# Two filter blocks transposed by their load instead of on TensorE, and one norm taken from PSUM, in a convolution-plus-FFN kernel

## The chip, the core and the metric

The kernel runs on one core of a Trainium2 chip. The metric is the time of one execution in device microseconds. The engines are TensorE (PE; its weight loads are PEld), VectorE (DVE), ScalarE (ACT), GpSimd (POOL) and SyncE (SP). SP and POOL also issue DMAs: SP's go through a hardware queue, POOL's through a software queue.

## The reference, cut to what matters

Sequence length S = 2048, width D = 640, FFN width F = 1728, everything bf16 in memory.

```python
h  = x + conv(layernorm(x), k, v)          # x is A_q
h2 = h + ffn(layernorm(h))

def conv(q, k, v):
    k_shift = causal 4-tap filter of k along S, per channel (shift_k)
    kv = k_shift * v
    y  = causal convolution of kv with ssm_k, per channel (a length-2S FFT in the reference)
    return q * (y + kv * ssm_D)

def ffn(x):
    return (silu(x @ w_gate) * (x @ w_up)) @ w_down
```

`ssm_k` is stored as [640, 2048], channels first. Its transform needs it with the sequence on the partitions, so each of its four blocks of 512 positions is transposed somewhere.

## The kernel before, in words

The sequence is cut into four blocks of N = 512 rows. For each block i the kernel forms kv (`kv`), transforms it with cosine and sine tables on TensorE (`xfwd`, tiles `X`, and `FO` for the odd half), multiplies it in the frequency domain with the filter blocks' transforms `C` (`prod`, VectorE, sums in `Y`), transforms back (`inverse`), normalises, and runs the FFN (`ffn`; for blocks 0 and 3 the gate and up products are in `gates`).

The four filter blocks come first. `kload(m)` loads block m as `kc[m]`, channels on the partitions. `ktrans(m)` transposes it on TensorE: two tasks of ten 128 x 128 transposes with the identity (L570), each followed by one eviction of 1280 columns from PSUM into `KT[m]`. `kfwd(m)` transforms `KT[m]` (L612); its results, even half in `C` or `R` and odd half in `KO`, are combined by VectorE butterflies (L583).

`kv(i)` loads K transposed with a transposing DMA (`tload`, L516, tile `kT`), applies the four taps with matmuls whose weights are the diagonal tiles `dg` and `dl` (L714, L719), and evicts. For block 0 it transposes back on TensorE (L733) and VectorE multiplies straight from PSUM into `vt` (L738). For the other blocks five more transposing DMAs make `kvo` and VectorE multiplies from there (L750). `dg` and `dl` are made by VectorE (L552, L556) from the identity and from `wcol`, the taps, which ACT's queue loads.

The second layernorm stands in `inverse`. For blocks in `ST` (0 to 2) one fused VectorE operation reads the inverse transform from PSUM, adds a row statistic, multiplies with x and sums (L876); POOL scales the sum (L880) and ScalarE squares and sums (L882). For block 3 ScalarE evicts from PSUM (L886), VectorE multiplies (L889), and ScalarE sums (L900) and squares (L902). All then use POOL for the power (L913). The normalised tile is transposed into `hnT` by four DMAs (L516), which the FFN's matmuls need.

The order of the work is written out by a table of numbers: `ORDER` holds, for each engine and for SP's queue, the numbers of the tasks in the order in which they are issued. Every engine works strictly in that order, and a task waits on semaphores for the tasks it depends on. PSUM tiles come from four units in turn. `VECTOR` lists the evictions that VectorE does instead of ScalarE, and `FILL` puts filler matmuls ahead of a task.

Of the kernel before, what the change touches and what calls it, by code (L numbers as in the profile page):

```python
# [10 lines left out]
ALU = mybir.AluOpType  # L11
# [11 lines left out]

class _Task:
    __slots__ = ("eng", "fn", "cost", "lat", "deps", "after", "succ", "npred", "ready", "end", "start",
                 "opens", "tiles", "idx", "clock", "sem", "seq", "dma", "name", "gap", "lock", "fill", "late", "pause", "alt")


class _Tile:
# [29 lines left out]
class _Graph:  # L59
# [38 lines left out]
    def add(self, eng, name, fn, cost, r=(), w=(), pr=(), pw=(), skip=(), lat=None, dma=None, after=(), lock=None):  # L98
        t = _Task()
# [131 lines left out]
    def emit(self, block):  # L231
# [5 lines left out]
        for t in self.glob:  # L237
# [32 lines left out]
            if t.dma is not None:  # L270
                t.sem = es.enter_context(nc.semaphore("s_d%d" % nd))
                nd += 1
                t.clock[t.sem] = 16
                prog[t.eng].append(lambda e, t=t: t.fn(e).then_inc(t.sem, 16))
            else:
                t.clock[t.eng] = t.idx
                prog[t.eng].append(lambda e, t=t, h=sems[t.eng]: t.fn(e).then_inc(h, 1))
        for t in self.glob:
            if t.dma is not None and not t.succ:
                prog["sp"].append(lambda e, t=t: e.wait_ge(t.sem, 16))  # L280

        @block.gpsimd
        def _(g):
# [23 lines left out]

ORDER = {
    "pe": """
# [7 lines left out]
    """,  # L317
    "act": """
# [11 lines left out]
    """,  # L330
    "dve": """
# [10 lines left out]
    """,  # L342
    "pool": """
        8 10 5 9 6 11 7 151 209 212 195 198 216 202 219 205 134 135 339 417 401 420 393 409 404 396 412 528 621 605 597 613
        624 600 608 616 770 775 780 785 732 827 809 836 818
    """,
    "sp": """
# [3 lines left out]
    """,  # L351
}

FILL = "20:6 313:8"

VECTOR = """
    59 83
"""

def bass_sequential_preLN__ssm_conv_h3__swiglu_ffn__prompt_kernel(  # L360
# [38 lines left out]
    with ExitStack() as es:  # L399
# [17 lines left out]
        NU = 5  # L417
# [8 lines left out]
        IE = sb("IE", o + 10400, [2, 2, D])  # L426
        o += 15520
        T = sb("T", o, [NU, 2, D])
        o += NU * 2560 - 10240
        kvo = sb("kvo", o + 10240, [4, D])  # L430
        FO = sb("FO", o + 10240, [2, 2, D])
# [16 lines left out]
        GA = sb("GA", o, [NC5, FA * P])  # L448
        UA = sb("UA", o + 8960, [NC5, FA * P])
        o += 17920  # L450
        GB = sb("GB", o, [NC5, FBK * P])
        UB = sb("UB", o + 7680, [NC5, FBK * P])
        PK = sb("PK", o + 15360, [NC5, P])
# [14 lines left out]
        epc = sb("epc", o + 544, [4], f32)  # L468
        assert o + 576 <= SBB + 16481 - A0, o + 576

        BN, DIRECT, D8, PT, BN2, ST, R4, PAIR, WARM, ACC, EA, KD, RD, LA, RA, HALF = (0,), (), (), (0,), (), (0, 1, 2), ('xf2',), True, 24, ((1, 3), (2, 3)), True, (2, 3), (), (1, 2, 3), (0, 1, 2), (0, 3)
        g = _Graph(nc, es)

        def cpe(n, k):
# [5 lines left out]
        def cdve(n):  # L480
            return 69 + n / 1.92
# [28 lines left out]
        def load(name, dst, src, nbytes, eng="sp", late=0, **kw):  # L510
            return g.add(eng, name, lambda e: e.dma_start(dst, src), 450, w=[dst], dma=(nbytes / 345.0, 0), lat=1900 + late, **kw)
# [24 lines left out]
        if WARM:  # L536
# [4 lines left out]
            def spin(e, pt=pt):  # L541
# [14 lines left out]
        g.add("dve", "dl", lambda e: e.tensor_tensor(out=dl[:], in0=id128, in1=w128, op=ALU.mult), 650,  # L556
              r=[wcol[:], ident[:]], w=[dl[:]])
# [4 lines left out]
        def ktrans(m):  # L562
            for jj in range(2):
                pt = g.tile("kt")

# [197 lines left out]

        ring_t = list(range(NU))
        ZB = sb("ZB", S[7], [2, 2, 2, D])

        def pair(u, v):
            return bass.AP(T[:].tensor, T[:].offset + 2 * D * u, [list(T[:].ap[0]), [D, 2], [(v - u) * 2 * D, 2], [1, D]])

        def prod(j, i):  # L770
            cm, nm = C[i - j], "p%d%d" % (j, i)
            for f2 in range(2):
                y = Y[:, f2]
                s = slice(f2, f2 + 3, 2)
                x, k = XH[j][:, s], cm[:, s]
                ksw = bass.AP(k.tensor, k.offset + D, [list(k.ap[0]), [4 * D, 2], [-D, 2], [1, D]])
                u = [ring_t.pop(0) for _ in range(4)]
                t1, t2 = pair(u[0], u[1]), pair(u[2], u[3])
# [382 lines left out]
```

## Time and profile before

| | |
|---|---|
| three runs | 262.37, 265.21, 268.7 us; median 265.21 |
| the profiled execution | 261.53 us, its span 259.5 us |
| granted TensorE clock | 1.0 |
| busy share of the span | PE 97%, PEld 65%, DVE 77%, ACT 75%, POOL 14% |
| first FFN matmul of block 0 | 55.96 us after the span's start |
| last filter matmul | up to 53.9 us |
| first inverse matmul of block 3 | 195.42 us |
| first FFN matmul of block 3 | 212.22 us |

Times in the views are microseconds from the span's start. The span is what the engines' instructions cover; the time of the execution is 2.0 us longer. The profiled execution is one of its own, 3.7 us below the median of the three runs. A busy share is an average over stages with different limits, so the busy time is better read stage by stage.

### The profile page before, as it was taken

To read this page: it belongs to the slowest core of one execution; us is meant where nothing else is said; L and a number is where in the kernel's file an instruction comes from. 1 tells how busy PE (TensorE), PEld (TensorE's weight loads), DVE (VectorE), ACT (ScalarE), POOL (GpSimd) and SP (SyncE) were. 2 spreads that over 40 slices of the span, in tenths; PEclk is the share of its full clock that TensorE was granted. 3 is DMA by queue.
4 is the path that set the end of the run, shared out by engine and by line. 5 is a ranking of instruction groups with operands and counts; after the bars stand their busy time and mean duration, and the time that the engine had idled before them with its cause. 6 is when DMAs were issued, how large, how long until landed. Compare 5 with 4: busy or idle time off the path is not lost.

```text
span 259.5 us, 4704 instructions
## 1 busy us (share of the span) xinstructions
PE 252.9 (97%) x1900; PEld 168.4 (65%) x1900; DVE 201.0 (77%) x292; ACT 194.8 (75%) x372; POOL 37.3 (14%) x49
## 2 busy tenths in 40 slices
PE   8999979999999999999999999999999999999996
PEld 5657645567888756644445666444456678888764
DVE  0799999999999999999999999999997010231222
ACT  2889999995698989669867798658977987654220
POOL 0001000434012141000030170310140101000000
PEclk9999999999999999999999999999999999999999
DMA  6995997999999653430031314993500030300005
GB/s 174 336 339 138 315 254 94 378 172 220 248 139 189 115 143 73 106 126 4 1 81 20 104 47 79 202 226 54 105 0 0 3 76 0 54 1 3 0 3 177
DMA packets 44792, 31.13 MB, mean 120 GB/s; under 512 B 32353, under 2 KB 41442, under 8 KB 44770
## 3 DMA queue, kind: packets, MB, share of 16 engines
q1 hardware_dynamic: 41968, 25.58, 38.9%
q0 software_dynamic: 2144, 5.24, 11.3%
q8 instruction: 15, 0.25, 0.4%
q10 hardware_dynamic: 658, 0.01, 0.1%
q14 instruction: 7, 0.06, 0.1%
HBM read 15.69 MB, written 2.62 MB: 71 GB/s over the span
## 4 chain that ended last, share of the span: by engine, by line
PE 86%; DMA 7%; ACT 5%; DVE 1%; SPq 0%; issue 0%
PE ps L1048 21%; PE ps L943 19%; PE ps L985 11%; PE ps L986 11%; PE ps L612 9%; PE ps L862 6%; DMA PK<-in_B_w_up_dram 3%; DMA kc<-in_A_ssm_k_dram 2%; PE ps L719 2%; DMA vt<-in_A_v_dram 2%; PE ps L1030 1%; ACT KT L504 1%; PE ps L1060 1%; ACT FO L504 1%; ACT X L504 1%; PE ps L649 1%
## 5 line engine op out<-in xcount | busy, mean ns | idle before, releaser
L1048 PE MATMUL ps<-Wd,GU 128*128 128x384 bf16 (+1 forms) x390 | 55.8, 299 | 0.0
L1048 PEld LDWEIGHTS ps<-Wd,GU 128*128 128x128 bf16 x390 | 37.9, 98 | 15.6 <-issue 0.5
L943 PE MATMUL ps<-hnT,GA 128*128 128x256 bf16 x140 | 31.1, 272 | 0.0
L943 PE MATMUL ps<-hnT,UA 128*128 128x256 bf16 x140 | 31.1, 273 | 0.0
L965 DVE TENSOR_TENSOR GU<-GU,ub 128x512 bf16<-128x512 bf16 (+1 forms) x28 | 10.9, 402 | 25.6 <-ACT GU L961 16.9
L781 DVE TENSOR_TENSOR T<-X,C 128x2560 bf16<-128x2560 bf16 x20 | 29.7, 1486 | 0.1
L782 DVE TENSOR_TENSOR T<-X,C 128x2560 bf16<-128x2560 bf16 x20 | 29.7, 1486 | 0.1
L943 PE MATMUL ps<-hnT,GB 128*128 128x256 bf16 x120 | 26.9, 273 | 0.5 <-DMA PK<-in_B_w_up_dram 0.5
L943 PE MATMUL ps<-hnT,UB 128*128 128x256 bf16 x120 | 26.9, 273 | 0.0
L961 ACT ACTIVATE GU<-ps 128x512 bf16<-128x512 f32 (+1 forms) x28 | 15.5, 568 | 14.8 <-PE ps L943 13.0
L985 PE MATMUL ps<-hnT,GA 128*128 128x512 bf16 x70 | 26.5, 379 | 0.0
L986 PE MATMUL ps<-hnT,UA 128*128 128x512 bf16 x70 | 26.5, 379 | 0.0
L1010 ACT ACTIVATE ub<-ps 128x512 bf16<-128x512 f32 (+1 forms) x30 | 17.1, 569 | 11.7 <-PE ps L986 6.3
L985 PE MATMUL ps<-hnT,GB 128*128 128x512 bf16 x60 | 22.7, 379 | 0.0
L986 PE MATMUL ps<-hnT,UB 128*128 128x512 bf16 x60 | 22.7, 379 | 0.0
L612 PE MATMUL ps<-KT,ftab 128*128 128x320 bf16 x128 | 19.5, 300 | 1.5 <-ACT KT L504 1.4
L963 ACT ACTIVATE ub<-ps 128x512 bf16<-128x512 f32 (+2 forms) x32 | 16.9, 545 | 3.6 <-DVE GU L965 1.8
L913 POOL TENSOR_TENSOR mv<-mv,half 128x1 f32<-128x1 f32 x16 | 14.1, 889 | 35.2 <-ACT mv L906 35.2
L833 POOL TENSOR_TENSOR st<-st,half 128x8 f32<-128x8 f32 x4 | 8.8, 2208 | 66.6 <-ACT st L827 66.6
L1008 ACT ACTIVATE GU<-ps 128x512 bf16<-128x512 f32 x26 | 15.0, 596 | 3.2 <-PE ps L986 3.1
L612 PEld LDWEIGHTS ps<-KT,ftab 128*128 128x128 bf16 x128 | 11.2, 98 | 8.4 <-ACT KT L504 1.9
L845 ACT ACTIVATE xh<-xh,st 128x640 bf16<-128x640 bf16 x16 | 14.3, 957 | 1.3 <-DVE st L835 1.2
(114 smaller groups left out, 499.4 us busy)
## 6 DMA issues: line engine op xcount, KB each, us to landing
kc<-in_A_ssm_k_dram SPq DMA_DIRECT2D x4, 640.0 KB, 5.6
xh<-in_A_q_dram SPq DMA_DIRECT2D x4, 640.0 KB, 5.8
vt<-in_A_v_dram SPq DMA_DIRECT2D x4, 640.0 KB, 4.3
Y<-ZB POOLq DMA_DIRECT2D x4, 640.0 KB, 6.2
out_dram<-xh SPq DMA_DIRECT2D x15, 160.0 KB, 1.9
Wd<-in_B_w_down_dram SPq DMA_DIRECT2D x1, 1280.0 KB, 7.5
C<-C POOLq DMA_DIRECT2D x1, 1280.0 KB, 12.3
C<-R POOLq DMA_DIRECT2D x1, 1280.0 KB, 10.8
```

The source lines that it names most:

```text
L612: last = e.matmul(pt.f(c, W), ftab[:, cs, j, f * P:(f + 1) * P], src[:, j, c * W:(c + 1) * W], start=(j == par), stop=(j == par + 2))
L781: g.add("dve", nm, lambda e, x=x, k=k, t1=t1: e.tensor_tensor(out=t1, in0=x, in1=k, op=ALU.mult), cdve(2560), r=[x, k], w=[t1])
L782: g.add("dve", nm, lambda e, x=x, k=ksw, t2=t2: e.tensor_tensor(out=t2, in0=x, in1=k, op=ALU.mult), cdve(2560), r=[x, k], w=[t2])
L862: last = e.matmul(pt.f(c, W), itab[:, cs, f, j, :], src[:, j // 2 if len(fs) == 1 else f, cs, c * W:(c + 1) * W], start=(f == 0 and cs == ...
L943: last = e.matmul(pt.flat(M, a + M * k), w[:, c, f0:f0 + P], hnT[:, c, ts], start=(c == 0), stop=(c == NC5 - 1))
L961: g.add("act", nm, lambda e, pt=pt, gv=gv, pg=pg: e.activation(out=gv, in_=pg(pt), func=ACTF.Silu, scale=gain), max(400, cact(n)), w=[gv], ...
L963: g.add("act", nm, lambda e, pt=pt, uv=uv, pu=pu: e.activation(out=uv, in_=pu(pt), func=ACTF.Copy, scale=gain), max(400, cact(n)), w=[uv], ...
L985: e.matmul(pt.f(0, N), wg[:, c, f0:f0 + P], hnT[:, c, :], start=(c == 0), stop=(c == NC5 - 1))
L986: last = e.matmul(pt.f(1, N), wu[:, c, f0:f0 + P], hnT[:, c, :], start=(c == 0), stop=(c == NC5 - 1))
L1008: g.add("act", nm, lambda e, pt=pt, gv=gv, a=ps_g, ts=ts: e.activation(out=gv, in_=pt.f(a[0], N, a[1])[:, ts], func=ACTF.Silu, scale=gain) ...
L1010: g.add("act", nm, lambda e, pt=pt, uv=uv, a=ps_u, ts=ts: e.activation(out=uv, in_=pt.f(a[0], N, a[1])[:, ts], func=ACTF.Copy, scale=gain) ...
L1048: last = e.matmul(pt.flat(c1 - c0, P + c0), slots[fb][:, at * P:(at + 1) * P], Wd[:, fb, c0:c1], start=(fb == 0 and not second), stop=(fb ...
```

## The change

Four things change.

1. Filter blocks 2 and 3 (`TK = (2, 3)`) are no longer loaded as `kc` and transposed on TensorE. A transposing DMA on SP's queue (`tload`) brings each into a new tile `kq`, in which position 128c + p lies in partition p. Four DMAs, each from 128 partitions into 32, then move it within SBUF to where `KT` is expected. With `TE = 'pool'` these are issued by POOL. The four share one semaphore, and a reader waits for 64 instead of 16 (`parts`).
2. `ST` is now (0, 1, 2, 3): block 3's second norm takes the same path from PSUM as the others.
3. `VECTOR` gives VectorE the first kv eviction of block 0 and one transform eviction of block 0, instead of one of `kt1` and one of `kf1`.
4. `ORDER` is new for every engine.

The code for `PL` (a different product) is added too, but `PL` is empty, so it is not used.

```diff
+        t.parts = 1
...
-                val = 16 if d.dma is not None else d.idx
+                val = 16 * d.parts if d.dma is not None else d.idx
...
-    59 83
+    21 165
...
-        BN, DIRECT, ..., ST, ... = (0,), (), (), (0,), (), (0, 1, 2), ...
+        BN, DIRECT, ..., ST, ..., PL, TK, TE = (0,), (), (), (0,), (), (0, 1, 2, 3), ..., (), (2, 3), 'pool'
...
+        box = {}
+
         def kload(m):
+            if m in TK:
+                q = sb("kq%d" % m, (GB_OFF, GB_OFF + 10240, kc23, kc23 + 5120)[m], [4, D])
+                tload("kTq%d" % m, q[:], A_ssm_k[:, N * m:N * (m + 1)], D, N, 2000)
+                def move(e, m=m, q=q):
+                    for c in range(4):
+                        last = e.dma_start(KT[m][32 * c:32 * c + 32, :, :], q[:, c, :])
+                        if c < 3:
+                            last.then_inc(box[m].sem, 16)
+                    return last
+
+                box[m] = g.add(TE, "kq%d" % m, move, 1800 if TE == "sp" else 4400, r=[q[:]], w=[KT[m][:]], dma=(2000, 0), lat=2000, lock=False)
+                box[m].parts = 4
+                return
             load("kc%d" % m, kc[m][:], A_ssm_k[:, N * m:N * (m + 1)].rearrange("(c p) s -> p c s", p=P), 655360)
 
         def ktrans(m):
+            if m in TK:
...
+                return
```

What the new tables move is seen in the order of the instructions. In these rows `kc_88` to `kc_91` are the filter blocks 0 to 3 as loaded, `KT_93` to `KT_96` the same transposed, `kq_119` and `kq_120` blocks 2 and 3 in the new tile, and `xh_72`, `xh_73` the buffers of x. A row ends with the size, and xN stands for N in a row.

SP's queue at the start of the program, before:

```order
L511 DMA kc_89<-in_A_ssm_k_dram 128x5x512
L511 DMA ident<-cst_id 128x192
L511 DMA kc_88<-in_A_ssm_k_dram 128x5x512
L511 DMA ftab<-cst_ftab 128x2048
L511 DMA xh_72<-in_A_q_dram 128x2560
L516 DMA_TRANSPOSE kT<-in_A_k_dram 128x5x512
L511 DMA vt<-in_A_v_dram 128x2560
L511 DMA kc_91<-in_A_ssm_k_dram 128x5x512
L511 DMA UA<-in_B_w_up_dram 128x5x896
L516 DMA_TRANSPOSE kT<-in_A_k_dram 128x5x528
L511 DMA kc_90<-in_A_ssm_k_dram 128x5x512
```

and now:

```order
L514 DMA ident<-cst_id 128x192
L519 DMA_TRANSPOSE kT<-in_A_k_dram 128x5x512
L514 DMA kc_88<-in_A_ssm_k_dram 128x5x512
L514 DMA vt<-in_A_v_dram 128x2560
L514 DMA ftab<-cst_ftab 128x2048
L514 DMA xh_72<-in_A_q_dram 128x2560
L519 DMA_TRANSPOSE kq_120<-in_A_ssm_k_dram 128x4x640
L514 DMA kc_89<-in_A_ssm_k_dram 128x5x512
L519 DMA_TRANSPOSE kT<-in_A_k_dram 128x5x528
L519 DMA_TRANSPOSE kq_119<-in_A_ssm_k_dram 128x4x640
L514 DMA itab<-cst_itab 128x2048
L514 DMA UB<-in_B_w_up_dram 128x5x768
```

The transposing load of block 0's K moves from sixth to second place, filter block 1 from first to eighth, and the two new transposing loads stand in seventh and tenth place. The weights UA and GA go behind block 1's load of v.

TensorE at the start, before (`gz` is the warm-up, `ident` alone a filler):

```order
L543 MATMUL ps<-gz 128x256 x24
L570 MATMUL ps<-ident,kc_89 128x128 x20
L570 MATMUL ps<-ident,kc_88 128x128 x20
L612 MATMUL ps<-KT_94,ftab 128x320 x32
L719 MATMUL ps<-kT,dg 64x512 x16
L612 MATMUL ps<-KT_93,ftab 128x320 x4
L714 MATMUL ps<-kT,dl 128x512 x4
L612 MATMUL ps<-KT_93,ftab 128x320 x4
L733 MATMUL ps<-ident,kT 128x128 x8
```

and now:

```order
L546 MATMUL ps<-gz 128x256 x24
L743 MATMUL ps<-kT,dg 64x512 x16
L251 MATMUL ps<-ident 128x192 x6
L743 MATMUL ps<-kT,dg 64x512 x16
L594 MATMUL ps<-ident,kc_88 128x128 x10
L757 MATMUL ps<-ident,kT 128x128 x8
L738 MATMUL ps<-kT,dl 128x512 x4
L594 MATMUL ps<-ident,kc_88 128x128 x10
L757 MATMUL ps<-ident,kT 128x128 x12
L636 MATMUL ps<-KT_93,ftab 128x320 x12
L636 MATMUL ps<-vt,ftab 128x320 x16
```

Block 0's kv work (`kT` with `dg`) now comes first, and filter block 1 only after block 0's filter and transform.

POOL from its last memset on, before:

```order
L530 MEMSET half 128x4
L833 ISA
L833 TENSOR_TENSOR st_0_105<-st_0_105,half 128x8
L880 TENSOR_SCALAR mv_109<-mv_109 128x1
L913 TENSOR_TENSOR mv_109<-mv_109,half 128x1
```

and now:

```order
L530 MEMSET kT 128x5x16
L570 DMA KT_96<-kq_120 32x4x640 x4
L570 DMA KT_95<-kq_119 32x4x640 x4
L901 ISA
L901 TENSOR_TENSOR st_0_105<-st_0_105,half 128x8
L948 TENSOR_SCALAR mv_107<-mv_107 128x1
```

Eight DMAs stand ahead of the power of block 0's first layernorm, block 3's filter before block 2's.

More of the change, by code (lines that the diff above doesn't have):

```diff
@@ L25 @@
     __slots__ = ("eng", "fn", "cost", "lat", "deps", "after", "succ", "npred", "ready", "end", "start",
-                 "opens", "tiles", "idx", "clock", "sem", "seq", "dma", "name", "gap", "lock", "fill", "late", "pause", "alt")
+                 "opens", "tiles", "idx", "clock", "sem", "seq", "dma", "name", "gap", "lock", "fill", "late", "pause", "alt", "parts")
 class _Tile:
@@ L272, in emit @@
                 nd += 1
-                t.clock[t.sem] = 16
+                t.clock[t.sem] = 16 * t.parts
                 prog[t.eng].append(lambda e, t=t: t.fn(e).then_inc(t.sem, 16))
@@ L279, in emit @@
             if t.dma is not None and not t.succ:
-                prog["sp"].append(lambda e, t=t: e.wait_ge(t.sem, 16))
+                prog["sp"].append(lambda e, t=t: e.wait_ge(t.sem, 16 * t.parts))
         @block.gpsimd
@@ L309 @@
     "pe": """
[7 rows of a table removed]
[7 rows of a table added]
     """,
     "act": """
[11 rows of a table removed]
[11 rows of a table added]
     """,
     "dve": """
[10 rows of a table removed]
[10 rows of a table added]
     """,
     "pool": """
-        8 10 5 9 6 11 7 151 209 212 195 198 216 202 219 205 134 135 339 417 401 420 393 409 404 396 412 528 621 605 597 613
-        624 600 608 616 770 775 780 785 732 827 809 836 818
+        10 6 11 8 7 9 5 65 63 145 189 196 210 199 192 203 213 206 128 129 333 395 411 387 398 403 414 390 406 522 599 615 591
+        607 602 594 610 618 765 770 775 780 726 816 800 819 808 803 824 811 827
     """,
     "sp": """
[3 rows of a table removed]
[3 rows of a table added]
     """,
@@ L428, in bass_sequential_preLN__ssm_conv_h3__swiglu_ffn__prompt_kernel @@
         T = sb("T", o, [NU, 2, D])
+        T_OFF, T_END = o, o + NU * 2560
         o += NU * 2560 - 10240
@@ L450, in bass_sequential_preLN__ssm_conv_h3__swiglu_ffn__prompt_kernel @@
         o += 17920
+        GB_OFF = o
         GB = sb("GB", o, [NC5, FBK * P])
@@ L557, in bass_sequential_preLN__ssm_conv_h3__swiglu_ffn__prompt_kernel @@
               r=[wcol[:], ident[:]], w=[dl[:]])
+        box = {}
         def kload(m):
+            if m in TK:
[10 more added lines that the diff above has]
+                return
             load("kc%d" % m, kc[m][:], A_ssm_k[:, N * m:N * (m + 1)].rearrange("(c p) s -> p c s", p=P), 655360)
         def ktrans(m):
+            if m in TK:
+                if m == 0:
+                    z = KT[0][0:1, 0, :]
+                    g.add("dve", "D", lambda e: e.tensor_tensor(out=z, in0=z, in1=drow[0:1, :], op=ALU.add), 410,
+                          r=[z, drow[0:1, :]], w=[z])
+                return
             for jj in range(2):
@@ L765, in bass_sequential_preLN__ssm_conv_h3__swiglu_ffn__prompt_kernel, with at_big, planes @@
         ZB = sb("ZB", S[7], [2, 2, 2, D])
+        ZH = {(j, f): sb("ZH%d%d" % (j, f), S[k], [4, 2, D]) for j, f, k in ((1, 0, 7), (2, 0, 2), (2, 1, 4))}
+        BIG = sb("BIG", 0, [T_END // 2])
         def pair(u, v):
             return bass.AP(T[:].tensor, T[:].offset + 2 * D * u, [list(T[:].ap[0]), [D, 2], [(v - u) * 2 * D, 2], [1, D]])
+        def at_big(off, *dims):
+            return bass.AP(BIG[:].tensor, BIG[:].offset + off // 2, [list(BIG[:].ap[0])] + [list(d) for d in dims])
+        def planes(j, i, f2, nm, x, k):
+            y = Y[:, f2]
+            yo = [S[6] + f2 * 5120, S[6] + f2 * 5120 + 2560]
+            if j:
+                home = ZH.get((j, f2)) if i == 3 else None
+                if home is None:
+                    un = [ring_t.pop(0) for _ in range(4)]
+                    ring_t.extend(un)
+                    u = [T_OFF + 2560 * v for v in un]
+                else:
+                    base = {(1, 0): S[7], (2, 0): S[2], (2, 1): S[4]}[j, f2]
+                    u = [base + 2560 * v for v in range(4)]
+            else:
+                un = [ring_t.pop(0) for _ in range(2)]
+                ring_t.extend(un)
+                a, b = (T_OFF + 2560 * v for v in un)
+                u = [a, yo[1], yo[0], b] if i % 2 else [yo[0], a, yo[1], b]
+            neg = u[0] if i % 2 else u[1]
+            ksw = bass.AP(k.tensor, k.offset + D, [list(k.ap[0]), [4 * D, 2], [-D, 2], [1, D]])
+            for p, q, kk in ((0, 1, k), (2, 3, ksw)):
+                d = at_big(u[p], (D, 2), ((u[q] - u[p]) // 2, 2), (1, D))
+                g.add("dve", nm, lambda e, d=d, kk=kk: e.tensor_tensor(out=d, in0=x, in1=kk, op=ALU.mult), cdve(2560), r=[x, k], w=[d])
+                if p == 0:
+                    z = at_big(neg, (1, 2 * D))
+                    g.add("dve", nm, lambda e, z=z: e.tensor_scalar(out=z, in0=z, scalar1=-1.0, scalar2=None, op0=ALU.mult), 430, r=[z], w=[z])
+            sets = ((2, 0), (3, 1)) if i % 2 else ((0, 2), (1, 3))
+            if j == 0:
+                sets = ((3, 0),) if i % 2 else ((1, 3),)
+            for a, b in sets:
+                z = at_big(u[a], ((u[b] - u[a]) // 2, 2), (1, 2 * D))
+                y2 = at_big(yo[0], (2 * D, 2), (1, 2 * D))
+                g.add("pool", nm, lambda e, y2=y2, z=z: e.dma_start(y2, z, accum_op=ALU.add, max_dma_last_dim=2560), 1100, r=[z, y2], w=[y2],
+                      dma=(4200, 0), lat=2000, lock=False)
@@ L775, in prod @@
                 x, k = XH[j][:, s], cm[:, s]
+                if (j, i) in PL:
+                    planes(j, i, f2, nm, x, k)
+                    if i == j:
+                        bfly("iv%d" % i, y[:, :, 0], y[:, :, 1], IE[:, f2], IO[:, f2], 2 * D)
+                    continue
                 ksw = bass.AP(k.tensor, k.offset + D, [list(k.ap[0]), [4 * D, 2], [-D, 2], [1, D]])
```

2 lines of the change are left out of this document (1 added, 1 removed), and 62 rows, old and new, of the table ORDER.

## The prediction

> **What bounds the kernel now.** I read the busy shares first, then the busy time by stage, then the chain of waits inside the stage that the change touches, and last the two queues that it loads (SP's and POOL's).
>
> ```profile
> PE 252.9 (97%) x1900; PEld 168.4 (65%) x1900; DVE 201.0 (77%) x292; ACT 194.8 (75%) x372; POOL 37.3 (14%) x49
> ...
> 6.00:56.00 50.00, 47.45 (x440) 30.23 (x440) 46.95 (x69) 47.49 (x72) 5.82 (x7) 1.00 0.98 257
> 56.00:196.00 140.00, 139.54 (x938) 87.39 (x937) 137.96 (x190) 110.36 (x226) 28.67 (x27) 1.00 0.51 109
> ...
> 196.00:212.40 16.40, 16.40 (x124) 11.09 (x122) 5.12 (x12) 14.36 (x30) 1.09 (x2) 1.00 0.14 31
> ```
>
> A window's row gives start and end, length, then the busy time of PE, weight loads, VectorE, ScalarE, POOL, the granted clock and the DMA share. "PE 97%" alone invites the conclusion that every matmul removed is time gained. The windows correct it. From 6 to 56 us (filters, block 0's convolution, block 1's transform) three engines are full together: PE 47.45, VectorE 46.95 and ScalarE 47.49 of 50. From 56 to 196 us PE and VectorE are full together: 139.54 and 137.96 of 140. Only after 196 us is VectorE free. So up to the last inverse transform (block 3's, 196 us) VectorE has 3.05 + 2.04 us idle in all. Whatever leaves VectorE's work as it is cannot bring that inverse more than 5.1 us forward, and TensorE alone cannot bring it forward at all.
>
> ```profile
> 28.82 1.13 ACT KT L504
> 29.95 1.83 ACT kT L504 x2
> 31.78 2.27 ACT KT L504 x2
> 34.10 7.11 PE ps L612 x48
> ```
>
> These are four pieces of the chain that ended last. The work that the change removes lies on it: the evictions of KT3 and KT2 hold ScalarE, and the filter matmuls start at 34.10 behind them.
>
> **What is removed, and what that frees.** Blocks 2 and 3 lose 40 TensorE transposes.
>
> ```profile
> 6.13 1.31 PE L570 MATMUL ps<-ident,kc 128*128 128x128 bf16 x20
> ...
> 34.10 2.08 PE L612 MATMUL ps<-KT,ftab 128*128 128x320 bf16 x14 [1.38 <-ACT KT L504]
> ...
> L504 ACT ACTIVATE KT<-ps 128x1280 bf16<-128x1280 bf16 x7 | 8.7, 1277 | 3.9 <-PE ps L570 3.9
> L494 DVE COPY KT<-ps 128x1280 bf16<-128x1280 bf16 x1 | 0.8, 817 | 0.0
> L738 DVE TENSOR_TENSOR vt<-ps,vt 128x1024 bf16<-128x1024 f32 x2 | 2.4, 1224 | 0.9 <-PE ps L733 0.9
> ```
>
> Twenty take 1.31 us, so PE sheds 2.6 us. Eight evictions become four. Before, seven ran on ScalarE and one on VectorE. Now all four run on ScalarE, which sheds 3 x 1.28 = 3.8 us, and some 0.9 us more as block 0's first kv eviction goes to VectorE. VectorE gives up a copy of 0.82 and takes a 1024-wide PSUM read; the nearest row, a multiply of that width from PSUM, takes 1.22. VectorE's work grows by 0.4 us: nothing is removed from the engine that has no time left. The PE wait of 1.38 us in front of the filter matmuls (transposes done, evictions not) does not vanish: it moves to kf1, whose transposes now stand directly ahead of it.
>
> **The new start.** Before, PE starts on filter 1 at 6.13. Now it starts on kv0, which needs dg.
>
> ```profile
> 6.11 1.23 DVE L552 TENSOR_TENSOR dg<-ident,wcol 128x1024 bf16<-128x1024 bf16 x1 [5.12 <-DMA ident<-cst_id]
> 7.25 0.69 DVE L556 TENSOR_TENSOR dl<-ident,wcol 128x512 bf16<-128x512 bf16 x1
> 9.94 0.82 DVE L496 TENSOR_SCALAR R<-ps 128x640 bf16<-128x640 f32 x1 [1.27 <-PE ps L612]
> ...
> 13.93 0.99 PE ps L719 x16
> 16.98 0.45 PE ps L733 x8
> 17.42 0.49 PE ps L250 x6
> 19.25 1.63 PE ps L612 x12
> ...
> wcol<-in_A_shift_k_dram ACTq DMA_DIRECT2D x1, 5.0 KB, 5.2
> ```
>
> Identity is loaded first now, but dg also needs wcol, which lands at 0.73 + 5.2 = 5.9, so dg ends near 7.34 as before. PE starts 1.2 us later. VectorE is done with dl at 7.94 and must wait for the second kv0 group: 7.34 + 0.99 + 0.49 (the six filler matmuls) + 0.99 = 9.8, an idle 1.9 us. Gone are its 1.27 here (the wait for kf1) and the 0.9 that it waited for kv0's transposes, which now run while it is at the eviction. So VectorE's path to the last inverse changes by 1.9 - 1.27 - 0.9 + 0.4 = +0.1 us. I take 0: one hole is filled and another opened.
>
> **The loads.** SP's queue gets two large transposing loads, kTq3 behind five loads and kTq2 behind kT1.
>
> ```profile
> 1.26 0.52 SPq L511 DMA_DIRECT2D ident<-cst_id  x1
> 2.86 0.58 SPq L511 DMA_DIRECT2D xh<-in_A_q_dram  x1
> 3.48 7.43 SPq L516 DMA_TRANSPOSE kT<-in_A_k_dram  x1
> 21.36 2.70 SPq L516 DMA_TRANSPOSE kT<-in_A_k_dram  x1
> ...
> xh<-in_A_q_dram SPq DMA_DIRECT2D x1, 640.0 KB, 7.8
> ...
> kT<-in_A_k_dram SPq DMA_TRANSPOSE x1, 9.4
> ...
> kT<-in_A_k_dram SPq DMA_TRANSPOSE x1, 4.8
> ...
> kc<-in_A_ssm_k_dram SPq DMA_DIRECT2D x4, 640.0 KB, 5.6
> ...
> 46.00:52.00 6.00, 5.85 (x49) 3.21 (x48) 5.68 (x12) 5.97 (x13) 3.00 (x4) 1.00 1.03 374
> ```
>
> The last figure of a queue row is the time from issue to landing. The same 640 x 512 transpose holds SP for 2.70 us when nothing is ahead of it (landed after 4.8) and for 7.43 when loads are: its issue ends at 10.91, just after the x0 load ahead of it landed (2.86 + 7.8 = 10.66), and it lands 2.0 later. I use that twice. Now kT0 has only ident ahead: issued 1.26 to 3.96, landed at 6.1, in time for dg. Behind it kc0, v0, ftab and x0 (2.4 MB) are issued by 6.1 and, at the 2.5 MB in about 10 us of before, landed near 13.5. kTq3 holds SP until then and lands at 15.6. kc1 follows at 14.0 and takes 5.6: 19.6, in time for its transposes near 21. kT1 is held to 19.6, landing at 21.6. kTq2 is issued then and lands 4.8 later if nothing holds it, and at most 1.5 more if kT1's last packets do: 24.4 to 25.9.
>
> **The moves.** POOL copies each filter in four DMAs of 160 KB. No plain copy within SBUF is in the trace, so I bound it.
>
> ```profile
> 63.59 1.49 POOL L690 DMA_DIRECT2D C<-C  x1 [3.69 <-DVE C L583]
> 162.77 1.26 POOL L795 DMA_DIRECT2D Y<-ZB  x1 [6.42 <-DVE ZB L787]
> 24.73 1.77 POOL L833 TENSOR_TENSOR st<-st,half 128x8 f32<-128x8 f32 x1 [23.54 <-ACT st L827]
> 42.48 3.50 ACT L845 ACTIVATE xh<-xh,st 128x640 bf16<-128x640 bf16 x4
> ...
> Y<-ZB POOLq DMA_DIRECT2D x4, 640.0 KB, 6.2
> out_dram<-xh SPq DMA_DIRECT2D x15, 160.0 KB, 1.9
> C<-C POOLq DMA_DIRECT2D x1, 1280.0 KB, 12.3
> ```
>
> Each issue holds POOL 1.26 to 1.49 us, four of them 5.0 to 6.0. The fourth of KT2 starts at 28.2 to 30.4. From issue to landing takes at least the 1.9 of a plain 160 KB store and at most the 6.2 of a four times larger accumulating move: KT2 is there between 30.1 and 36.6. PE needs it after kv0 (3 x 0.99, transposes 1.1, fillers 0.5), kt0 and kt1 (1.31 each), kf0, xf0 and kf1 (4.35 each at 1.63 for 12), kv1 (2.97) and four groups of kf3 (2.17): 25.4 us from 7.34, plus the wait of 1.4, is 34.1. The middle of arrival is 33; what is later than 34.1 is paid one for one, since PE issues in order and VectorE's next butterflies wait for kf2. I take 1.0 us, from the earlier part of what is left since the size is that of the store, and keep 0 to 2.5. POOL's power for block 0's first norm waits behind these issues (till 32 at most); before, it ran at 24.73 and ScalarE came to use it at 42.48, so some 8 us of cover remain. The late UA, GA and GB (3.2 MB behind v1, which waits for block 0's inverse) take about 9 us at the 374 GB/s that 46 to 52 us shows; from 43 they are in by 54, with about 2 us of cover: 0.
>
> [...]
>
> **Block 3's second norm.** Per tile, ScalarE's PSUM read and its sum, and VectorE's multiply, give way to one fused VectorE operation and a small POOL one.
>
> ```profile
> L876 DVE SCALAR_TENSOR_TENSOR xh<-ps,st,xh 128x640 bf16<-128x640 f32 x12 | 10.2, 881 | 0.1
> L886 ACT ACTIVATE qo<-ps,st 128x640 bf16<-128x640 f32 x4 | 3.1, 782 | 0.0
> L889 DVE TENSOR_TENSOR xh<-xh,qo 128x640 bf16<-128x640 bf16 x4 | 2.0, 488 | 8.1 <-ACT xh L845 8.1
> ```
>
> ScalarE sheds 4 x 0.78 = 3.1 us and four passes that sum a tile; VectorE takes 4 x (0.88 - 0.49) = 1.6 more, and is busy 5.12 of 16.40 us there. PE is busy 16.40 of 16.40 there with block 2's output matmuls. So it counts 0; without that cover the shorter chain would gain at most some 2 us, as the four tiles overlap. The new order inside the FFN blocks counts 0 for the same reason: the same matmuls, PE full.
>
> **The sum**, against the profiled execution (span 259.5, time 261.53, so 2.0 around the span): VectorE's path 0, KT2's arrival +1.0, the rest 0: span 260.5, time 262.5. That execution is 3.7 below the median of the runs shown, 265.21; on their scale I predict 266.2. Those runs spread from 262.37 to 268.7, so about 2% (5.3 us) is what a measurement of this kernel can tell from no change.
>
> **Rivals.** (a) KT2 comes late, and it is slower. One mechanism: a transposing load that holds SP until all ahead of it has landed, then four POOL copies that land like the 1280 KB moves (12.3) and not like a store. From 30.4 that is 42.7, 8.6 us after PE wants it: time 261.5 + 8.6 = 270.1, or 273.8 on the runs' scale. It is slower by over 2% once KT2 lands after about 39. For it: the 7.43 us row, and no cover on PE or VectorE. Against: kTq2 is not behind plain loads, and 160 KB is small. Chance 0.30. (b) Faster: the front is held by ScalarE's evictions, as the chain says, and VectorE's holes close with them. All 3.05 us idle before 56 us would go, less the 0.4 added: time 258.9, 262.5 on the runs' scale; with some of the idle after 56 us, 260. For it: 28.82 to 34.10 of the chain is ScalarE. Against: VectorE, 46.95 of 50 busy, works through the same list. Chance 0.15. [...] Chance 0.06. My forecast has 0.49.
>
> **Chances and range.** Faster by over 2% (under 259.9): only the far end of (b), 0.06. Slower by over 2% (over 270.5): most of (a), some of (c), a little of the forecast for costs unseen: 0.25 + 0.02 + 0.05 = 0.32. Within 2%: 0.62. The forecast's own range is 265.2 (no wait) to 267.7 (2.5 us). For eight in ten I go to (b)'s 262.5 and a little below, and to near the end of (a): 262.0 to 273.0.
>
> **What would show it.** Right: no KT evictions near 30 us; PE's first kv0 matmul at 7.3; VectorE idle some 2 us before its first kv0 eviction, then full until 195 to 197; the first block-3 inverse matmul within 1.5 us of 195.4; the gate matmuls of block 0 within 2 us of 56. Wrong: a PE wait of over 3 us on KT in front of kf2 or kf3 (a, c); or block 3's inverse at 193 or earlier (b), which needs VectorE's idle time to shrink, the step I am least sure of.

## The result, and the profile after

The changed kernel takes 276.77 us (median of 4, 275.8 to 279.47) against 264.54 us (median of 4, 262.37 to 268.7) for the kernel before on the same chip: 1.0521 times as long, 95% interval 1.0463 to 1.0579. It is slower, and it lies outside the predicted range of 262.0 to 273.0. The profiled execution took 276.92 us, with a span of 275.1 and a granted clock of 0.975 (before: 261.53, 259.5 and 1.0). Ratios below leave disturbed executions out, so a ratio may differ from that of two medians, most in a_pk.

First the busy shares and the busy time by stage of the changed kernel (start and end, length, then PE, weight loads, VectorE, ScalarE, POOL, granted clock, DMA share, GB/s):

```profile
PE 255.8 (93%) x1860; PEld 167.9 (61%) x1860; DVE 203.4 (74%) x297; ACT 186.5 (68%) x356; POOL 43.9 (16%) x61
...
6.00:56.00 50.00, 39.75 (x329) 24.46 (x330) 37.45 (x56) 36.89 (x56) 8.57 (x12) 0.93 1.04 239
56.00:196.00 140.00, 134.90 (x929) 84.94 (x927) 131.28 (x180) 104.53 (x210) 28.34 (x28) 0.98 0.58 122
36.00:42.00 6.00, 1.16 (x8) 0.53 (x7) 5.26 (x10) 2.75 (x6) 2.05 (x1) 0.78 1.19 113
42.00:47.00 5.00, 5.00 (x24) 2.92 (x23) 1.65 (x2) 2.21 (x4) 0.00 (x0) 0.58 1.04 261
84.00:90.00 6.00, 1.57 (x12) 1.01 (x11) 4.95 (x7) 1.09 (x2) 0.00 (x0) 0.76 1.19 187
90.00:96.00 6.00, 6.00 (x39) 4.57 (x38) 1.61 (x4) 2.50 (x6) 0.00 (x0) 0.67 1.15 259
```

TensorE does 40 matmuls fewer and is yet "busy" 2.9 us longer. In the first stage three engines that were full together now have 10 to 13 us of holes each. The four short rows find the two places: TensorE is nearly empty in 36 to 42 and 84 to 90, and right behind each hole it is full but at a clock of 0.58 and 0.67. The timeline of TensorE gives the two waits (start, busy time, idle time before it and what ended it):

```profile
35.54 1.31 PE L636 MATMUL ps<-KT,ftab 128*128 128x320 bf16 x8 [0.25 <-ACT R L507]
41.70 3.63 PE L636 MATMUL ps<-KT,ftab 128*128 128x320 bf16 x13 [4.84 <-DMA KT<-kq]
...
84.48 0.27 PE L1011 MATMUL ps<-hnT,UA 128*128 128x256 bf16 x1
89.18 0.37 PE L1011 MATMUL ps<-hnT,GB 128*128 128x256 bf16 x1 [4.43 <-issue]
```

The milestones say how much each is worth. Block 0's first gate matmul is at 64.93 instead of 55.96 (9.0 later), block 1's first inverse matmul at 101.32 instead of 86.12 (15.2 later, so 6.2 more), block 3's at 211.08 instead of 195.42, and the span ends 15.6 later. Behind block 1's inverse nearly nothing is added.

What is late in the front is seen on SP's queue, then POOL's, then in the DMA issues (last figure: median us from issue to landing):

```profile
6.99 7.70 SPq L519 DMA_TRANSPOSE kq<-in_A_ssm_k_dram  x1
15.36 4.83 SPq L519 DMA_TRANSPOSE kT<-in_A_k_dram  x1
20.23 7.49 SPq L519 DMA_TRANSPOSE kq<-in_A_ssm_k_dram  x1
30.93 9.97 SPq L519 DMA_TRANSPOSE kvo<-kT  x5
...
18.39 2.41 POOL L570 DMA_DIRECT2D KT<-kq  x4 [17.12 <-DMA kq<-in_A_ssm_k_dram]
30.18 2.17 POOL L570 DMA_DIRECT2D KT<-kq  x4 [9.37 <-DMA kq<-in_A_ssm_k_dram]
...
KT<-kq POOLq DMA_DIRECT2D x8, 160.0 KB, 7.4
kq<-in_A_ssm_k_dram SPq DMA_TRANSPOSE x2, 10.4
```

The second transposing load of a filter holds SP for 7.49 us though only another transposing load (block 1's K) stands directly ahead of it, POOL gets to its moves at 30.18, and KT2 is there at 41.7. Block 1's K is late too: it lands 11.8 us after its issue, and TensorE waits 1.42 us for it before 27.17. The second place is the queue around PK, the last two weight columns of the gates:

```profile
79.21 0.60 SPq L514 DMA_DIRECT2D Wd<-in_B_w_down_dram  x1
79.85 0.58 SPq L514 DMA_DIRECT2D PK<-in_B_w_gate_dram  x1
80.48 6.33 SPq L519 DMA_TRANSPOSE kvo<-kT  x2
...
PK<-in_B_w_up_dram SPq DMA_DIRECT2D x1, 80.0 KB, 2.4
PK<-in_B_w_gate_dram SPq DMA_DIRECT2D x1, 80.0 KB, 9.2
```

The new order issues the gate half of PK only at 79.85, behind three of block 2's transposes. It lands 9.2 later, at 89.05, and TensorE goes on at 89.18. TensorE's row names no releaser for that wait ("issue"); that it is PK rests on these two times and on the run a_pk below.

### The profile page after: what moved, and what is told of

It reads as the page before. It is cut to its first block, busy times and chain, and to the rows that moved or that the text cites. A ratio compares the mean times of both kernels' runs of the same rounds, so it can differ in the third digit from the quotient of the medians.

```text
span 275.1 us, 4626 instructions
## 1 busy us (share of the span) xinstructions
PE 255.8 (93%) x1860; PEld 167.9 (61%) x1860; DVE 203.4 (74%) x297; ACT 186.5 (68%) x356; POOL 43.9 (16%) x61
## 4 chain that ended last, share of the span: by engine, by line
PE 55%; DVE 17%; DMA 12%; ACT 9%; issue 3%; SPq 2%; POOL 2%; DVEq 0%
PE ps L1011 21%; PE ps L1116 11%; PE ps L1054 5%; PE ps L1053 5%; PE ps L636 5%; DVE T L850 4%; DMA KT<-kq 4%; DMA kq<-in_A_ssm_k_dram 4%; PE ps L930 3%; DMA Y<-ZB 3%; DVE T L849 3%; DMA vt<-in_A_v_dram 2%; DVE xh L944 2%; SPq L519 1%; PE ps L1098 1%
## 5 line engine op out<-in xcount | busy, mean ns | idle before, releaser
L1011 PE MATMUL ps<-hnT,GA 128*128 128x256 bf16 x140 | 31.9, 277 | 0.0
L1011 PE MATMUL ps<-hnT,GB 128*128 128x256 bf16 x120 | 27.8, 278 | 4.4 <-issue 4.4
L1011 PE MATMUL ps<-hnT,UA 128*128 128x256 bf16 x140 | 31.8, 276 | 0.0
L636 PE MATMUL ps<-KT,ftab 128*128 128x320 bf16 x128 | 22.0, 322 | 7.7 <-DMA KT<-kq 4.8
L1011 PE MATMUL ps<-hnT,UB 128*128 128x256 bf16 x120 | 27.8, 278 | 0.0
L1029 ACT ACTIVATE GU<-ps 128x512 bf16<-128x512 f32 (+1 forms) x28 | 15.2, 562 | 16.0 <-PE ps L1011 8.2
L636 PEld LDWEIGHTS ps<-KT,ftab 128*128 128x128 bf16 x128 | 12.4, 104 | 16.6 <-issue 5.1
L944 DVE SCALAR_TENSOR_TENSOR xh<-ps,st,xh 128x640 bf16<-128x640 f32 x16 | 13.8, 882 | 8.2 <-PE ps L930 7.2
L948 POOL TENSOR_SCALAR mv<-mv 128x1 f32<-128x1 f32 x16 | 10.8, 675 | 36.5 <-DVE xh L944 36.5
```

The costliest lines, as they stand in the source:

```text
L636: last = e.matmul(pt.f(c, W), ftab[:, cs, j, f * P:(f + 1) * P], src[:, j, c * W:(c + 1) * W], start=(j == par), stop=(j == par + 2))
L944: g.add("dve", nm, lambda e, pt=pt, x2=x2, s=s, j=j, m=m: e.scalar_tensor_tensor(out=x2, in0=pt.f2(W), scalar=s[:, 3, j:j + 1], in1=x2, op ...
L1011: last = e.matmul(pt.flat(M, a + M * k), w[:, c, f0:f0 + P], hnT[:, c, ts], start=(c == 0), stop=(c == NC5 - 1))
L1029: g.add("act", nm, lambda e, pt=pt, gv=gv, pg=pg: e.activation(out=gv, in_=pg(pt), func=ACTF.Silu, scale=gain), max(400, cact(n)), w=[gv], ...
```

## The experiments

Four theories came out of this. R: the new route of filter blocks 2 and 3 makes KT2 late. Q: PK's place on SP's queue causes the second wait. T: a TensorE that has waited 4 to 5 us runs slowly for some 5 us more. O, the rival to all: the new order as such is slower, and the waits only show it. "Gates" is the start of block 0's first gate matmul in the traced execution of each run. Each ratio is to the kernel before on the same chip; the medians of two rows can come from different chips.

| run | what it is | median us | ratio to before, 95% | gates at |
|---|---|---|---|---|
| a_pk | changed, PK's halves together | 270.54 | 1.0194 (1.0082 to 1.0305) | 66.8 |
| a_tkoff | changed, transposes on TensorE again | 272.57 | 1.0387 (1.0334 to 1.0440) | 61.4 |
| a_tkoff_pk | both of these | 266.31 | 1.0152 (1.0111 to 1.0194) | 61.4 |
| b_tk | before, with the new route alone | 275.45 | 1.0494 (1.0422 to 1.0566) | 70.9 |
| a_pk_sp | a_pk, moves issued by SP | 269.37 | 1.0242 (1.0190 to 1.0295) | 64.1 |
| a_direct_pk | a_pk, KT2 and KT3 by plain loads | 262.58 | 1.0011 (0.9981 to 1.0041) | 57.3 |
| b_st3 | before, with block 3's new norm | 264.76 | 1.0077 (1.0033 to 1.0120) | 56.4 |
| a_fill | changed, fillers in the two waits | 274.96 | 1.0426 (1.0339 to 1.0512) | 62.9 |
| b_direct | before, KT2 and KT3 by plain loads | 262.89 | 1.0008 (0.9962 to 1.0053) | 58.7 |
| a_pk_sp2 | a_pk_sp, SP's queue rearranged | 279.97 | 1.0678 (1.0612 to 1.0744) | 64.9 |
| a_pk_flat | a_pk, moves into the same 128 partitions | 263.53 | 1.0058 (1.0023 to 1.0092) | 57.6 |
| a_pk_spread | a_pk, moves into every fourth partition | 263.30 | 1.0034 (1.0000 to 1.0067) | 58.9 |

**PK's place (a_pk).** Of SP's table one number moves (220 is the gate half, 221 the up half):

```diff
-... 221 223 501 509 505 224 220 506 502 222 ...
+... 221 220 223 501 509 505 224 506 502 222 ...
```

> One edit to the changed kernel: SyncE issues the gate half PK (task 220) right behind the other half (task 221), ahead of the three transposes of block 2 behind which the new order had put it. Theory Q (the place of PK on SyncE's queue is what makes TensorE wait 4.43 us at 89.18 for block 0's gates, and the lower granted clock behind that wait costs some 2 us more): 271 us, 5 to 6 less than the changed kernel; the inverse of block 1 starts near 96 instead of 101.3. Rival (TensorE's wait there only passes on the 9.0 us that the front is late, or another operand of the gates is as late): 275 to 277, no change.

It took 270.54 us, 6.2 less. Its four times spread from 266.14 to 272.74, and the traced one is the longest: there TensorE waits 7.2 us for KT2, not 4.84, and the gates begin 1.9 us later than in the changed kernel. From them to block 1's inverse, which begins at 96.32, it is 29.5 us instead of 36.4. The gate half now lands 3.3 after its issue, and the wait is gone from TensorE's list:

```profile
PK<-in_B_w_gate_dram SPq DMA_DIRECT2D x1, 80.0 KB, 3.3
...
90.00:96.00 6.00, 6.00 (x58) 5.37 (x56) 5.87 (x11) 4.08 (x10) 2.11 (x1) 1.00 1.06 240
```

The clock in 90 to 96 is 1.00 again and 58 matmuls go through where 39 did. Q holds. It is one number moved among some 900.

**The transposes back on TensorE (a_tkoff, a_tkoff_pk).**

```diff
-        ..., (0, 3), (), (2, 3), 'pool'
+        ..., (0, 3), (), (), 'pool'
```

In the tables kTq3 and kTq2 become kc3 and kc2, and the transposes with their evictions stand ahead of the first halves that read them.

> The changed kernel with filter blocks 2 and 3 loaded plainly and transposed on TensorE again (four transposing groups, evicted on ScalarE, put ahead of the first halves that read them); the rest of the new order, PK's place too, stays. Theory R (the new route makes KT2 land at 41.7, and that is the 9.0 us by which block 0's gates start late): 268 to 270, with the first gate matmul near 56 to 58, since some 3 us of transposes come back on TensorE. Rival O (the new order as such is late in the front, kv0 first and fewer operands at hand): 275 to 279, the first gate matmul still near 64.

> Both edits at once: filter blocks 2 and 3 on TensorE again, and PK behind its other half; left of the change are the new order elsewhere and block 3's second norm from PSUM. Theories R and Q together: 261 to 265, no difference from the kernel before. Rival O: 269 to 272, since only PK's part comes back.

The first took 272.57, the second 266.31; both lie between R and O. PK's part is again 6.3 us (272.57 to 266.31), and here the four times of each run lie within 1 us, so this is its firmer size. But 1.5%, some 4 us, stays above the kernel before. The timeline of VectorE in the second run shows a wait that can account for most of it:

```profile
38.96 0.82 DVE L608 TENSOR_TENSOR R<-R,KO 128x1280 bf16<-128x1280 bf16 x1
42.80 0.16 DVE L904 TENSOR_TENSOR st<-st 128x4 f32<-128x4 f32 x1 [3.01 <-POOL st L902]
```

VectorE waits 3.01 us for block 0's first norm. POOL's power for it stands behind a ScalarE step that begins at 40.72, behind the four evictions that I had put ahead of it. I put this down to their place and not to the new order: without these evictions (a_direct_pk) that step begins at 36.11 and VectorE does not wait. No run puts them elsewhere, so this is argued, not shown.

**The route in the old order (b_tk).** The kernel before with `TK = (2, 3)` alone: the transposing loads stand where the plain ones stood, the moves are POOL's first DMAs.

> The kernel before, in its own order, with the new route alone for filter blocks 2 and 3: their transposing loads stand where the plain loads stood on SyncE, the moves within SBUF are the first thing that GpSimd does behind its memsets, the four transposing groups and their evictions are gone. Theory R: KT2 lands after 40, so 270 to 275, 6 to 10 more than before. Rival (the route does no harm where the order does not put its loads behind others): 260 to 265.

275.45 us, 4.9% more: the route alone costs nearly as much in the old order as the whole change does (5.2%). TensorE's list of waits names two that were not there:

```profile
PE ps L637 <- DMA KT<-kq: 8.3, 1, 8.3
PE ps L744 <- DMA kT<-in_A_k_dram: 6.0, 1, 6.0
```

The second is block 1's K, a transposing load that has nothing to do with the filters except that it stands on the same queue as they do.

**The moves from SP's queue (a_pk_sp, a_pk_sp2).** `TE = 'sp'`; the moves stand right behind kTq2 on SP.

```diff
-... kTq2 itab UB kvt1 ...          (POOL: kq3 kq2)
+... kTq2 kq3 kq2 itab UB kvt1 ...
```

> The changed kernel with PK behind its other half, and the two moves within SBUF issued by SyncE right behind the second filter block's transposing load, in place of GpSimd: no copy runs beside a transposing load. Theory C (GpSimd's copy of block 3, whose packets took 640 to 800 ns each at 21 to 25 us, holds up the transposing loads behind it): the load of block 2 is released near 25 instead of 27.5, KT2 lands near 33, TensorE does not wait for it, 262 to 265. Rival L (the transposing load of block 2 waits for the loads ahead of it whatever GpSimd does): the load still holds SyncE to 27.5, KT2 lands near 36, 265 to 268. Rival M (a copy of 128 into 32 partitions takes 7 to 11 us from any queue): KT2 at 40 or later and the transposes of the filter's output held on SyncE behind it, 270 or more.

SP's queue in this run:

```profile
20.25 2.75 SPq L520 DMA_TRANSPOSE kq<-in_A_ssm_k_dram  x1
23.04 5.23 SPq L571 DMA_DIRECT2D KT<-kq  x8
...
29.53 11.49 SPq L520 DMA_TRANSPOSE kvo<-kT  x5
...
47.05 0.58 SPq L515 DMA_DIRECT2D vt<-in_A_v_dram  x1
```

The first half of theory C came out: with no move in flight beside it, the transposing load holds SP for 2.75 us, not 7.49, and TensorE waits only 1.0 us for KT2. But the time was 269.37. The moves now stand ahead of block 1's five transposes, which hold SP for 11.49 us, so that v1 is issued at 47.05 and TensorE waits 5.0 us for the product with it. I then tried to get the queue out of its own way (itab ahead of kT1, v1 ahead of kT2, UB behind GA):

> The changed kernel with PK behind its other half, both moves issued by SyncE behind the second transposing load, and SyncE's queue rearranged around them: itab's load behind kc1, v1's load ahead of kT2's transposing load, UB's behind GA. It is meant to take away the 5.0 us that TensorE waited for the product with v1 when the moves went through SyncE, because v1 was issued at 47.05 behind kT2. Theory C (the copies do no harm once nothing that is needed stands behind them): 262 to 265, v1 issued near 43, no wait of TensorE over 1.5 us. Rival (a copy of 5 to 6 us holds every transposing load behind it on SyncE wherever it stands): the five transposes of the filter's output still hold SyncE to 40 or more, 266 to 270.

It was a miss, 279.97 us, slower than the change itself. SP's queue and TensorE's waits show why:

```profile
50.26 2.85 SPq L515 DMA_DIRECT2D GB<-in_B_w_gate_dram  x1
53.62 4.80 SPq L520 DMA_TRANSPOSE hnT<-qo  x1
...
PE ps L1012 <- DMA hnT<-qo: 10.6, 2, 5.5
```

Four weight loads now stand directly ahead of the transposes of block 0's normalised tiles, and those wait for them. I had counted only what stands ahead of v1. Neither theory had named this wait.

**What the route could bring at best (a_direct_pk, b_direct).** KT2 and KT3 are filled by plain loads of as many bytes; their transposition is left out.

```diff
-                q = sb("kq%d" % m, ...)
-                tload("kTq%d" % m, q[:], A_ssm_k[:, N * m:N * (m + 1)], D, N, 2000)
...
+                d = KT[m][:].rearrange("p a d -> p (a d)").rearrange("p (x s) -> p x s", s=N)
+                load("kTq%d" % m, d, A_ssm_k[:, N * m:N * (m + 1)].rearrange("(p x) s -> p x s", x=5), 655360)
```

> The changed kernel with PK behind its other half, and KT2 and KT3 filled by plain loads of the same bytes at the place of the transposing ones; the transposition of filter blocks 2 and 3 is left out, and so are the moves. It shows what the new order is worth when the route costs nothing. Theory R (all of the front's loss is the route's): 257 to 261, a gain against the kernel before of some 3 us of transposes. Rival O (the new order loses in the front by itself, as the 266.3 of the order with the transposes on TensorE says): 263 to 266.

> The kernel before, in its own order, with KT2 and KT3 filled by plain loads of the same bytes at the places of the loads of filter blocks 2 and 3; their transposition is left out, so TensorE has some 3.2 us less work and ScalarE four evictions less, and nothing is copied. It is the most that any route past TensorE can bring in this order. Theory V (VectorE is full beside TensorE, so TensorE's relief alone brings next to nothing, as the 262.6 of the same thing in the new order says): 261 to 263. Rival P (TensorE's and ScalarE's relief counts in full where the order is right): 258 to 260.

262.58 and 262.89 us, in both orders no difference from before that these runs can tell; the intervals leave room for 0.4% less and 0.5% more. So the new order loses nothing measurable once PK is in place and KT2 is on time, and taking the transposes off TensorE gains nothing measurable either. The timeline of TensorE in the second run shows where the freed time goes:

```profile
30.88 6.93 PE L628 MATMUL ps<-KT,ftab 128*128 128x320 bf16 x48 [0.52 <-ACT kT L508]
41.09 4.45 PE L922 MATMUL ps<-IO,itab 128*128 128x320 bf16 x16 [3.27 <-DVE IO L599]
```

Before, the same 48 filter matmuls stood at 34.10 and were followed at once. Now they begin 3.2 us earlier, TensorE then waits 3.27 us for VectorE's IO, and block 0's inverse starts at 41.09, to the hundredth where it started before. VectorE is busy 10.93 of the 11 us from 30 to 41 there.

**The norm alone (b_st3).** The kernel before with `ST = (0, 1, 2, 3)`.

> The kernel before with one part of the change alone: block 3's second norm taken from PSUM on VectorE (four fewer evictions and four fewer mean passes on ScalarE, the four STTs on VectorE in place of four multiplications, one negation more). The prediction's 0 for it: 262 to 264, no difference from before. Rival (VectorE is full to 196 us, so its 0.5 us longer operations show, or ScalarE's relief behind 196 shows): 260 to 261 or 265.

264.76 us, 0.3 to 1.2% more. From block 3's first inverse matmul to the end it is 64.6 us, before 64.1, so the norm as such shows nothing. What is lost lies ahead of it: to fit the operations in I had to put four of ScalarE's steps ahead of FFN evictions, and TensorE waits 2.4 and 1.6 us for such an eviction (`ACT ub L1079`). That is 4.0 of the 5.8 us by which block 3's inverse is later in this trace, which is of the longest of the ten executions (267.7 us). The part of this that is the norm's own stays open, but in the changed kernel itself the same stretch is 64.0 us.

**Fillers in the two waits (a_fill).**

```diff
-FILL = "20:6 313:8"
+FILL = "20:6 313:8 92:55 250:50"
```

> The changed kernel with 55 small idle matmuls (128x192) ahead of the first half of filter block 2 and 50 ahead of the gates' pieces that wait for PK, into the PSUM tile that is about to be written: they fill TensorE's two waits and change nothing else. Theory T (an idle TensorE of 4 to 5 us is followed by 5 us at a granted clock of 0.58 to 0.67, which costs some 2 us each time): 272 to 274, clock 1.0 in the stretches 42 to 47 and 90 to 96. Rival (the clock has another cause, or what follows is not bound by TensorE): 275 to 278.

Its four times, 272.1 to 276.9, do not tell it from the changed kernel; the intervals of the two ratios overlap. The trace does tell the clock's part. It is of the shortest of the four, the only one with a mean clock of 1.0 (the others have 0.988 to 0.994). Two windows and the row behind the first wait:

```profile
42.00:47.00 5.00, 5.00 (x39) 3.51 (x38) 0.79 (x2) 4.48 (x8) 0.00 (x0) 1.00 0.98 256
90.00:96.00 6.00, 6.00 (x58) 5.37 (x56) 5.49 (x11) 4.85 (x11) 1.67 (x1) 1.00 1.17 214
...
36.45 4.71 PE L251 MATMUL ps<-ident 128*128 128x192 bf16 x55 [0.20 <-ACT KO L508]
41.23 3.43 PE L637 MATMUL ps<-KT,ftab 128*128 128x320 bf16 x24
```

The same 24 filter matmuls took 5.60 us in the changed kernel, behind an empty wait, and 3.43 behind fillers: 2.2 us. From the first gate matmul to block 1's inverse it is 33.7 us instead of 36.4: 2.7. So T holds in the trace. The changed kernel's windows have means of 0.58 over 5 us and 0.67 over 6 us, behind waits of 4.84 and 4.43 us; in finer ones the clock is still 1.00 from 36.86 to 39.20, inside the first wait, and 0.50 from 39.50 to 46.00. A shorter wait, 3.27 us in b_direct, was followed by a clock of 0.50 as well (last section).

**Why the move is slow (a_pk_flat, a_pk_spread).** The same eight DMAs of the same bytes, from the same queue; only the partitions they write differ:

```diff
-                        last = e.dma_start(KT[m][32 * c:32 * c + 32, :, :], q[:, c, :])
+                        last = e.dma_start(KT[m][:, c, :], q[:, c, :])           # a_pk_flat
+                        last = e.dma_start(KT[m][c:P:4, :, :], q[:, c, :])       # a_pk_spread
```

> The changed kernel with PK behind its other half, and the four pieces of each move written to the same 128 partitions that they are read from, not to 32 each; the filter's positions in blocks 2 and 3 then stand in another order than the computation needs, all else is as it was. Theory W (the move is slow because each piece goes from 128 into 32 partitions): the pieces land 2 to 4 us after their issue, KT2 near 34, 264 to 267. Rival S (any copy within SBUF of these 640 KB takes that long, or the landing waits for the transposing loads): KT2 still lands near 41, 269 to 272.

> As the run with the moves into the same 128 partitions, but each piece again goes from 128 partitions into 32, every fourth one of the 128 instead of 32 that lie side by side; the filter's positions in blocks 2 and 3 then stand in another order than the computation needs. Theory N (32 partitions side by side are the narrow place, so pieces spread over all 128 are as quick as the wide ones): packets of about 200 ns, KT2 there before TensorE wants it, 262 to 265. Rival T (it is the number of written partitions, 32, wherever they lie): packets of 400 to 800 ns, KT2 near 41, 269 to 272.

263.53 and 263.30 us: by the medians the 7 us of the route are gone (3 to 9, as a_pk's times spread), and 0.3 to 0.6% above the kernel before is left. TensorE waits for KT2 in neither. In a_pk_flat SP is held for 4.34 us and POOL's second set is issued at 26.54; in both, the pieces land after 4.8 us in the median, not the 2 to 4 that theory W had said. The queue rows of the DMA view over the same 6 us (21 to 27 us from the start), of the changed kernel and then of the two runs:

```profile
q0 software_dynamic: 192, 0.66, 75.4%
...
q0 software_dynamic: 192, 0.66, 29.6%
...
q0 software_dynamic: 192, 0.66, 29.8%
```

```profile
19.92 4.34 SPq L520 DMA_TRANSPOSE kq<-in_A_ssm_k_dram  x1
...
26.54 2.12 POOL L571 DMA_DIRECT2D KT<-kq  x4 [6.09 <-DMA kq<-in_A_ssm_k_dram]
KT<-kq POOLq DMA_DIRECT2D x8, 160.0 KB, 4.8
```

One block's move is 192 packets, 0.66 MB in all, in each case; these rows are of block 3's. Into 32 neighbouring partitions it took 75.4% of 16 engines' 6 us, into all or into every fourth 29.6 and 29.8%: 2.5 times as much. For block 2's move, in 27 to 45 us, the shares are 28.4% in the changed kernel, 38.4% in a_pk and 9.0% in both runs: 3.2 and 4.3 times. This is the time that the packets took; from issue to landing the medians are 7.4 and 4.8 us, 1.5 times. It is not the number of partitions written, since each piece writes 32 in a_pk_spread too, but that they lie side by side: 75.4% against 29.8%. What makes neighbours slower no run shows.

## Why the prediction was wrong, and where it was right

- **KT2's arrival, the term of +1.0 us.** This is the step that failed first. TensorE wanted KT2 at 36.9 (34.1 forecast; 1.42 of these 2.8 us is its wait for block 1's K), and KT2 came at 41.7 and not at 33: a wait of 4.84 us in place of the 1.0. Two sizes under it were wrong. *The loads*: kTq2 was issued at 20.23 (19.6 forecast) but held SP 7.49 us, not 2.7, and landed 9.7 after its issue, at 30, not 24.4 to 25.9. The prediction counted on "kTq2 is not behind plain loads", and left out that block 3's move runs at that very time: with the move wide it is 4.34, with the move behind it 2.75. *The moves*: bounded by a 160 KB store (1.9) and a 640 KB accumulating move (6.2), they landed after 7.4 in the median and 9.8 at most. Neither row writes 32 neighbouring partitions, and the prediction had the 128-into-32 in front of it without asking what it costs.
- **"What is later than 34.1 is paid one for one."** Too little: the slower clock behind the wait adds 2.2 us to a wait of 4.84.
- **The order inside the FFN blocks, 0, "the same matmuls, PE full".** This step failed too, by some 6.2 us. The matmuls were the same, but a DMA that feeds them had been moved behind three transposes on SP. The prediction followed SP's queue to UA, GA and GB, which it had in by 54 us, and not to PK behind them.
- **VectorE's path 0, and TensorE's relief worth nothing.** Right to within some 0.5%, and the firmest result: 1.0011 and 1.0008 with the transposition gone altogether.
- **The start.** Wrong in its pieces, right in the sum. The taps landed 2.1 us after their issue (5.2 before), dg ran at 2.82 and not at 6.11, TensorE's first kv0 matmul came at 6.82 (7.3 forecast), and VectorE then sat idle 4.88 us, not 1.9. It sat idle longer because it was done with dl sooner; the end of the wait, 9.53, is near the 9.8 forecast. The sum that gave VectorE's 0 had counted 1.9, so that its pieces cancel is partly luck. The runs with KT2 on time show that it costs nothing measurable.
- **UA, GA, GB late, 0, and block 3's norm, 0.** Right: no wait on those weights appears, and from block 3's inverse to the end it is 64.0 us, before 64.1.
- **POOL's issues at 1.26 to 1.49 us.** Too dear: four took 2.41 and 2.17 us, some 0.55 each, the second four while VectorE was busy 10.93 of the 11 us from 25 to 36. The chances count (c), a KT2 made late by slow issues, with 0.06, and 0.02 of it in the 0.32: no run shows such issues, and the eight here took 0.55 to 0.77 us each.
- **Rival (a)** came nearest to what happened in the front: KT2 at 42.7 by its sum, 41.7 measured. That its 8.6 us lie near the 9.0 measured is partly luck: the wait was 4.84, and it had neither the slower clock behind it nor the 2.8 us by which TensorE came to it later. The copies were slow for another reason than the one it borrowed from the 1280 KB moves. It had 0.30 where the forecast had 0.49. The reason given against it, that 160 KB is small, was wrong. And its 273.8 lacks PK, so the measured 276.8 lies above even this rival. Rival (b) did not show: VectorE's idle time grew.

## What to carry to other kernels

Price a move within SBUF by the partitions that it writes and not by its bytes alone: into 32 neighbours it took the DMA engines 2.5 to 4.3 times what it took into 32 spread ones, and the transposing load in flight beside it held its queue 7.49 us instead of the 4.34 beside a move into all 128. When an order is new, follow each queue to its end and ask of every load what now stands ahead of it and who waits: the place of one weight load of 80 KB cost 6.2 us, the narrow moves some 7. And before pricing a relief of one full engine, ask what another full engine does with it: here 3.2 us of TensorE turned into 3.27 us of waiting for VectorE.

## What was not expected of the hardware

- A move into 32 neighbouring partitions slowed what ran beside it. With it in flight a transposing load held its queue 7.49 us, with the same bytes moved to all partitions 4.34 (a_pk_flat), with none in flight 2.75 (a_pk_sp). That the writes to those partitions block the queue is argued from these three, not shown by itself.
- The clock fell after a single wait of 3.27 us too. In b_direct the clock is 1.00 from 30 to 36 us, and the 5 us behind that wait ran at 0.50:

```profile
36.00:41.00 5.00, 1.82 (x13) 0.83 (x11) 4.96 (x7) 5.00 (x9) 0.00 (x0) 0.91 0.84 128
41.00:46.00 5.00, 4.91 (x19) 2.83 (x20) 3.73 (x5) 1.62 (x3) 0.00 (x0) 0.50 0.61 137
```

In this execution, the longest of its ten (265.05; they go from 261.24), the gates begin at 58.7, 2.7 later than before, though the inverse starts at the same time. Of the ten, four have a mean clock of 1.0 (261.24 to 263.23 us), five 0.993 (262.77 to 263.61) and this one 0.987. Here 3.2 us of relief on TensorE became a wait of 3.27 us and gates that begin 2.7 us later; whether the other five lost their clock at the same wait, no trace shows.
